# Dilated heads two tokens per transpose, XT reordered in its copy out of PSUM, and no filler matmuls, in a fused attention and soft-MoE kernel

## The chip, the cores and the metric

The kernel runs on one core of one Trainium2 chip. The metric is device time in microseconds (us) for one execution. The engines are TensorE (PE in the profile, with PEld for its weight loads), VectorE (DVE), ScalarE (ACT), GpSimd (POOL) and SyncE (SP). They run side by side and wait for one another by semaphores. POOL issues all input loads here, SP the stores.

## What is computed

Attention with a sliding window, and then a soft mixture of experts on its result. There are 8 batches, 8 heads, 576 tokens and 64 values per head.

```python
scores = scale * np.matmul(q, k.transpose(0, 1, 3, 2))
rel = pos[:, None] - pos[None, :]
mask_plain = (rel >= 0) & (rel < 32)                            # heads 0 to 3
mask_dil = (rel >= 0) & (rel < 128) & (rel % 4 == 0)            # heads 4 to 7
attn_out = softmax(where(mask, scores, -1e9)) @ v
x = attn_out.transpose(0, 2, 1, 3).reshape(4608, 512)           # tokens x (heads, values)

logits = x @ phi                                                # 4608 x 32 slots
d = softmax of logits over tokens;  slot_input = d.T @ x        # 8 experts x 4 slots
h = np.maximum(slot_input[e] @ w1[e], 0.0)                      # 512 -> 1024
slot_out[e] = h @ w2[e]                                         # 1024 -> 512
c = softmax of logits over slots;   out = c @ slot_out          # 4608 x 512
```

A dilated head's query sees only keys whose distance is a multiple of four. If its tokens are regrouped by their index modulo four, it becomes a plain window of 32 within each group of 144 tokens.

## The kernel before

**Units.** The attention is done in eight units u. A unit is one pair of batches and one type of head: even units hold the four plain heads, odd units the four dilated ones (`ty = u % 2`). Its q, k and v are loaded by POOL into one of three staging slots `stg`, 96 rows (q, k, v times batch times a run of 72 tokens) on 96 partitions for each of two halves of the heads.

**Stages of a unit.** Each stage is a call of a function `st_...`, which adds operations to a list.

- `st_T` (four calls per unit): PE transposes `stg` into PSUM against an identity (L515), and ACT copies two banks to `TT` (L532), which holds values on partitions and tokens along the free dimension. For dilated heads the copy puts the tokens in groups modulo four. Two 64-column transposes, one for each half of the heads, fill the two halves of PSUM's partitions. POOL's next load into this staging slot waits for these transposes.
- `st_S` (six calls): scores (L550), ACT's exponential (L557) and DVE's mask (L565) for four blocks of 96 queries against 128 keys, of two heads that lie on the two halves of the partitions. `win` gives the window of `TT` for a block.
- `st_V` (four calls): PE transposes v back (L575), DVE copies it (L580).
- `st_P` (four calls): probabilities times v, with a column of ones for the sum (L603); DVE takes the reciprocal (L612) and scales into `XB` (L614), tokens on partitions.
- `st_X` (four calls): PE transposes `XB` (L631), and DVE or ACT copies it to `XT` (L640, L641), values on partitions. For dilated heads `XT` is in the grouped order of tokens.
- `st_L` (odd units only, once per batch): logits from the `XT` of both types (L660), eight matmuls of 192 and 384 columns. For the dilated half the output goes to PSUM with a step of four, so that its tokens come out in natural order. ACT takes the exponential (L665), DVE copies parts of it (`expX`, L672), PE transposes it per block (L692), DVE copies (`ET`, L696), and PE adds the slot inputs into one PSUM bank (L705).

**Tail.** The slot inputs are copied (L747), folded (L752), copied again (`siT`, L757). Then come the first expert layer (L772), the token sums (L809), a transpose of h (L790) with copies (L799), the second expert layer (L830, in three parts by when weights land), its scaling (L844, L848), and 18 output blocks (L869, copies L872 and L875, stores L880). Expert weights are loaded by POOL into `WD`, and the last nine into `stg` and `TT` as those come free.

**Order.** `Prog.schedule` is a planner. It takes each operation's cost in microseconds, its key (a due time from `due`, units 13.1 us apart) and its dependences, and lays every engine's order down at build time. Calls of neighbouring units interleave. An operation with two engines named (`("dve", "act")`) goes to the one that can start it first. A change of PE's weight shape has a cost of its own in the planner (`mode`). PSUM has seven banks in the planner's pool, of which pairs are taken by most stages. Where PE would stand still for over 0.4 us by the plan and the plan's time is past `FILL[0]`, the planner puts in matmuls whose result nobody reads (`filler`, L889).

## Time and profile before

| | |
|---|---|
| median of 3 runs | 189.43 us |
| lowest of them | 189.08 us |
| the profiled execution | 190.36 us, of which the span from first to last instruction is 188.6 us |
| PE busy | 142.1 us (75%), 2872 matmuls |
| DVE, ACT, POOL busy | 110.1 us, 94.2 us, 35.8 us |
| read from HBM, written | 61.93 MB, 9.44 MB |
| PE's granted clock, mean | 0.926 of full |
| matmuls whose result is unused (L889) | 32, 8.9 us busy |

A row of a group of instructions gives line, engine, operation, output and input with partitions and elements, the count, then busy time and the mean duration of one in ns, and the idle time of the engine before them with its releaser. Rows in order of time give start, length, engine and line. Rows of windows give a stretch, the busy time of the engines in it with counts, the clock granted to PE, the share of the DMA engines' time, and GB/s. The chain is followed back from the last instruction; "issue" in it is time in which an engine waited for nothing that the profile shows.

### The profile page before, as it was taken

The page shows a single profiled execution, that of the slowest core. Times are in us where ns is not written, and L with a number is a line of the kernel's source. Part 1 is how long each engine was busy: PE and PEld are TensorE (multiplying, and loading weights), DVE is VectorE, ACT ScalarE, POOL GpSimd, SP SyncE. Part 2 cuts the span into 40 slices and gives each one's busy share as a digit, 9 for nine tenths or more (in the row PEclk, how much of TensorE's full clock was granted, in tenths as well). Part 3 has the DMA queues.
Part 4 walks back from the last instruction along what each step waited for, and adds up shares of the span by engine and source line. Part 5 has one row for each costly group of instructions (what it writes and reads, how often), then busy time and mean ns, then how long its engine had stood idle before and what let it go on. Part 6 is the DMA issues. An engine that isn't in the chain of part 4 may idle for free.

```text
span 188.6 us, 6342 instructions
## 1 busy us (share of the span) xinstructions
PE 142.1 (75%) x2872; PEld 104.4 (55%) x2872; DVE 110.1 (58%) x256; ACT 94.2 (50%) x136; POOL 35.8 (19%) x72
## 2 busy tenths in 40 slices
PE   0028879599987878998949799887899999996000
PEld 0028668487766757776837677675664658311000
DVE  6820794496687359569528966948943130699000
ACT  2006857456675655675649476478321020699000
POOL 7980603301500420440020020010400000000000
PEclk9999999669999978999996999999699999999855
DMA  5999999999999999999999999949999950199998
GB/s 76 211 215 211 213 212 218 213 216 215 212 210 220 216 208 221 213 212 215 216 216 208 219 219 217 208 99 151 219 215 214 215 109 3 60 405 405 407 403 322
DMA packets 7898, 40.83 MB, mean 216 GB/s; under 512 B 1856, under 2 KB 1856, under 8 KB 4416
## 3 DMA queue, kind: packets, MB, share of 16 engines
q0 software_dynamic: 4752, 30.94, 79.9%
q1 hardware_dynamic: 3120, 9.50, 12.8%
q8 instruction: 22, 0.36, 0.7%
q14 instruction: 4, 0.03, 0.0%
HBM read 61.93 MB, written 9.44 MB: 378 GB/s over the span
## 4 chain that ended last, share of the span: by engine, by line
PE 50%; DVE 26%; issue 5%; DMA 5%; ACT 4%; POOL 1%; DVEq 0%; POOLq 0%
PE ps L515 13%; DVE PT L565 8%; PE ps L660 6%; DVE XB L614 6%; PE ps L631 6%; DVE WD L875 5%; DVE VN L580 5%; DMA stg<-in_v_dram 5%; PE ps L889 4%; PE ps L575 4%; PE ps L603 3%; PE ps L550 3%; PE ps L830 3%; ACT PT L557 2%; PE ps L772 2%
## 5 line engine op out<-in xcount | busy, mean ns | idle before, releaser
L532 ACT ACTIVATE TT<-ps 128x864 f32<-128x864 f32 x32 | 28.3, 894 | 30.0 <-PE ps L515 30.0
L515 PE MATMUL ps<-ident,stg 96*64 96x96 bf16 x1152 | 32.4, 215 | 14.4 <-DMA stg<-in_v_dram 12.9
L557 ACT ACTIVATE PT<-ps 128x768 bf16<-128x768 f32 x48 | 37.4, 810 | 10.0 <-PE ps L550 10.0
L515 PEld LDWEIGHTS ps<-ident,stg 96*64 96x64 bf16 x1152 | 28.3, 116 | 16.6 <-DMA stg<-in_v_dram 12.9
L614 DVE TENSOR_TENSOR XB<-ps,RV 96x768 bf16<-96x768 f32 x32 | 30.2, 945 | 0.5
L580 DVE COPY VN<-ps 128x768 bf16<-128x768 bf16 x32 | 17.6, 549 | 19.2 <-PE ps L575 19.1
L550 PE MATMUL ps<-TT 64*128 64x96 bf16 x384 | 17.9, 221 | 4.5 <-issue 2.5
L603 PE MATMUL ps<-VN,PT 128*128 128x65 bf16 x384 | 19.0, 203 | 2.8 <-DVE VN L580 1.1
L575 PE MATMUL ps<-ident,TT 128*128 128x128 bf16 x192 | 18.4, 238 | 2.3 <-issue 2.3
L603 PEld LDWEIGHTS ps<-VN,PT 128*128 128x128 bf16 x384 | 15.7, 104 | 5.3 <-DVE VN L580 1.5
L396 POOL DMA_DIRECT2D stg<-in_q_dram x16 | 8.4, 526 | 51.3 <-PE ps L515 50.5
L631 PE MATMUL ps<-ident,XB 96*128 96x96 bf16 x192 | 13.6, 214 | 5.1 <-DVE XB L614 3.0
L575 PEld LDWEIGHTS ps<-ident,TT 128*128 128x128 bf16 x192 | 12.5, 107 | 7.9 <-issue 5.3
L631 PEld LDWEIGHTS ps<-ident,XB 96*128 96x128 bf16 x192 | 10.4, 103 | 8.1 <-issue 3.7
L550 PEld LDWEIGHTS ps<-TT 64*128 64x128 bf16 x384 | 10.8, 102 | 7.2 <-ACT PT L557 1.6
L641 ACT ACTIVATE XT<-ps 128x576 bf16<-128x576 bf16 x16 | 10.4, 648 | 8.2 <-PE ps L631 8.2
L640 DVE COPY XT<-ps 128x576 bf16<-128x576 bf16 x16 | 7.3, 455 | 11.4 <-PE ps L631 11.4
L565 DVE TENSOR_TENSOR PT<-PT,mask_d 128x768 bf16<-128x768 bf16 x24 | 12.8, 535 | 0.9 <-ACT PT L557 0.5
L660 PE MATMUL ps<-XT,phi_pad 128*128 128x192 bf16 (+1 forms) x64 | 13.0, 362 | 0.0
L565 DVE TENSOR_TENSOR PT<-PT,mask_p 128x768 bf16<-128x768 bf16 x24 | 12.7, 541 | 0.0
L612 DVE RECIPROCAL RV<-ps 96x12 f32<-96x12 f32 x32 | 7.1, 223 | 7.9 <-PE ps L603 7.8
L425 POOL DMA_DIRECT2D stg<-in_moe_w_dram x6 | 3.2, 534 | 42.1 <-PE ps L515 42.1
(75 smaller groups left out, 161.5 us busy)
## 6 DMA issues: line engine op xcount, KB each, us to landing
WD<-in_moe_w_dram POOLq DMA_DIRECT2D x7, 1024.0 KB, 25.4
out_dram<-WD SPq DMA_DIRECT2D x14, 512.0 KB, 5.0
stg<-in_moe_w_dram POOLq DMA_DIRECT2D x6, 1024.0 KB, 15.2
stg<-in_q_dram POOLq DMA_DIRECT2D x16, 288.0 KB, 13.2
stg<-in_k_dram POOLq DMA_DIRECT2D x16, 288.0 KB, 14.9
stg<-in_v_dram POOLq DMA_DIRECT2D x16, 288.0 KB, 17.5
TT<-in_moe_w_dram POOLq DMA_DIRECT2D x2, 1024.0 KB, 14.5
out_dram<-stg SPq DMA_DIRECT2D x4, 512.0 KB, 5.1
```

The source lines that it names most:

```text
L515: i_ = t.transpose(bankb2(pt, a)[64 * hx:64 * hx + 64, 96 * kk:96 * kk + 96], src[:, hx, c, :], ident[0:96, 0:96])
L532: return ac.activation(d, sv, ACTF.Copy)
L550: i_ = t.matmul(pair(sc)[:, hx, QB * x:QB * x + QB], win(u, 1, h01, blk_, bpar)[64 * hx:64 * hx + 64], win(u, 0, h01, blk_, bpar)[64 * hx: ...
L557: op("act", lambda ac: ac.activation(sbt(pt)[:, 0:768].rearrange("p (x n) -> p x n", x=2), pair(sc)[:, :, 0:384], ACTF.Exp, scale=SCALE), ...
L565: return dv.tensor_tensor(p_, p_, m.unsqueeze(1).to_broadcast([128, 2, 384]), AluOp.mult)
L575: i_ = t.transpose(bankb(pv)[:, 128 * m:128 * m + 128], win(u, 2, h01, m, bpar), ident[:, :])
L580: op("dve", lambda dv: dv.tensor_copy(sbt(vn)[:, :, :, 0:64], bankb(pv)[:, 0:768].rearrange("p (m x d) -> p m x d", m=6, x=2)), r=[pv], w= ...
L603: i_ = t.matmul(pair(po)[:, hx, 65 * m:65 * m + 65], sbt(pts[i])[:, o_:o_ + 128], sbt(vn)[:, m, hx, 0:65], start=True, stop=True)
L614: op("dve", lambda dv: dv.tensor_tensor(sbt(xb)[:].rearrange("p m (x h d) -> p h x m d", x=2, h=2)[:, h01], pv()[:, :, :, 0:64], sbt(rv)[: ...
L631: i_ = t.transpose(bankb(px)[:, QB * m:QB * m + QB], sbt(xb)[:, m, 128 * x:128 * x + 128], ident[0:QB, 0:QB])
L641: return en.activation(d, s_, ACTF.Copy)
L660: i_ = t.matmul(o_, phi_pad[:, c].rearrange("p j i -> p (j i)"), rhs, start=c == 0, stop=c == 3)
```

## The change

It has three parts, and new costs for the planner.

1. In odd units `st_T` transposes 96 x 128 at a time: two tokens next to each other in one head, 18 transposes per call instead of 36. The halves of the partitions then hold even and odd tokens instead of two heads. `win` finds its windows accordingly, ACT's copy goes to one half of `TT`, and `st_P` puts its results at the places in PSUM from which `XB` gets the same layout of values.
2. The copy of a dilated `XT` out of PSUM reads with a step and writes in a row, so that `XT` is in natural order. The logits' matmuls then read and write in a row for both types. The steps in `expX` and in the transposes of the exponential (L692) follow the new order of blocks.
3. `FILL[1]` is zero, so the planner puts in no filler.

```diff
-FILL = (125.0, 1e9)
+FILL = (125.0, 0)
...
     def win(u, t, h01, i, bpar):
-        base = (2 * t + h01) * S + QB * i - (HALO if t else 0)
+        if u % 2 == 0:
+            base = (2 * t + h01) * S + QB * i
+        else:
+            base = (6 * (i // 3) + 2 * t + h01) * 288 + QB * (i % 3)
+        base -= HALO if t else 0
...
     def st_T(u, j):
+        two = stg[0:96, s, :].rearrange("r (x c d) -> r x c d", x=2, d=128)
...
                 for kk in range(9):
-                    c = 18 * j + 9 * a + kk if ty == 0 else 4 * (9 * a + kk) + j
+                    if ty:
+                        c = 2 * (9 * a + kk) + j % 2
+                        i_ = t.transpose(bankb2(pt, a)[:, 96 * kk:96 * kk + 96],
+                                         two[:, j // 2, c, :], ident[0:96, 0:96])
+                        continue
+                    c = 18 * j + 9 * a + kk
...
-        op("pe", pe, r=[b_id, b_stg[s]], w=[pt], alloc=[pt], cost=0.86, mode="h",
+        op("pe", pe, r=[b_id, b_stg[s]], w=[pt], alloc=[pt], cost=0.86 if ty == 0 else 0.75,
+           mode="h" if ty == 0 else "f",
...
-                d = t32.rearrange("p (s n) -> p s n", s=6)[:, :, 144 * j:144 * j + 144]
+                d = t32[:, 1728 * (j // 2):1728 * (j // 2) + 1728].rearrange(
+                    "p (s n) -> p s n", s=6)[:, :, 144 * (j % 2):144 * (j % 2) + 144]
...
     def st_P(u, g):
-                for hx in range(2):
-                    o_ = 384 * hx + QB * x
-                    i_ = t.matmul(pair(po)[:, hx, 65 * m:65 * m + 65],
+                for half in range(2):
+                    o_ = 384 * half + QB * x
+                    bk, po_ = (half, m) if ty == 0 else (m // 3, 3 * half + m % 3)
+                    i_ = t.matmul(pair(po)[:, bk, 65 * po_:65 * po_ + 65],
...
     def st_X(u, bpar, x):
             d, s_ = sbt(xt)[:, x, :], bankb(px)[:, 0:S]
+            if ty:
+                s_ = s_.rearrange("p (y x s) -> p s x y", y=2, x=2)
+                d = d.rearrange("p (s x y) -> p s x y", y=2, x=2)
...
-           cost={"dve": 0.38, "act": 0.55}, key=k0 + 0.6)
+           cost={"dve": 0.38 if ty == 0 else 0.8, "act": 0.57}, key=k0 + 0.6)
...
     def st_L(b, u):
-                    if c < 2:
-                        rhs = sbt(x0)[:, c, lo:hi]
-                    else:
-                        o_ = o_.rearrange("p (i r) -> p r i", r=4)
-                        rhs = sbt(x1)[:, c - 2, :].rearrange("p (r i) -> p r i", r=4)[
-                            :, :, lo // 4:hi // 4]
+                    rhs = sbt((x0, x1)[c // 2])[:, c % 2, lo:hi]
...
-                n = expT[:, S * b:S * b + S].rearrange("p (i x y) -> p x y i", x=2, y=2)
+                n = expT[:, S * b:S * b + S].rearrange("p (i y x) -> p x y i", x=2, y=2)
...
-                    f_ = QB * m
-                    o_ = 4 * (f_ % 144) + f_ // 144
+                    o_ = m // 3 + (4 * 48 + 2 if m % 3 else 0)
```

The planner's costs also change for the scores (0.2 to 0.22), L603 (0.41 to 0.46), L631 (0.28 to 0.31), L692 (0.5 to 0.56) and L752 (1.4 to 1.9). These numbers alter no instruction, only the order that the planner lays down.

## Prediction

> **What bounds the kernel now.** I read the page first: the slices, then the chain that ended last.

> ```profile
> span 188.6 us, 6342 instructions
> ...
> DMA  5999999999999999999999999949999950199998
> ...
> PE 50%; DVE 26%; issue 5%; DMA 5%; ACT 4%; POOL 1%; DVEq 0%; POOLq 0%
> ```

> The DMA engines are full almost throughout, yet half of the chain is PE. Two holes in the DMA line (slice 27, and 33 to 35) reconcile this. I asked for the first by a window and by order of time.

> ```profile
> 122.00:127.00 5.00, 4.38 (x140) 3.78 (x139) 2.67 (x5) 3.75 (x5) 0.38 (x1) 1.00 0.57 118
> ...
> 126.62 1.06 POOL L425 DMA_DIRECT2D stg<-in_moe_w_dram  x2 [15.65 <-PE ps L515]
> ...
> 163.54 15.62 SPq L880 DMA_DIRECT2D out_dram<-WD  x14
> ```

> The first row gives the stretch, the five engines' busy time, PE's clock, the DMA share and GB/s: over those five microseconds DMA moves at 0.57. The queue runs dry because the weights that go into unit 7's staging slot cannot be issued before unit 7's transposes (L515) are done, at 126.6. The second hole lies ahead of the first store at 163.54, where PE finishes the expert layers with every weight on the chip. After it comes only output, 188.6 - 163.5 = 25 us of DMA that the change leaves alone. So the end is set by when PE gets through eight units of attention and the tail behind them; loading fits around it. A microsecond less on PE is a microsecond less at the end, as long as DVE and ACT keep up.

> **The change part by part.** *Logits (L660).* Half of a batch's eight matmuls write PSUM with a step of four today; afterwards all write in a row.

> ```profile
> 45.99 1.64 PE L660 MATMUL ps<-XT,phi_pad 128*128 128x192 bf16 x8
> ...
> 47.41 0.46 PE L631 MATMUL ps<-ident,XB 96*128 96x96 bf16 x6
> ...
> 145.50 1.04 PE L889 MATMUL ps<-mask_p,ident 128*128 128x512 bf16 x4
> ...
> L889 PE MATMUL ps<-mask_p,ident x32: 376/379/634, 136.0 to 161.8; 128*128 128x512 bf16 x32
> ```

> From the first logits matmul to the next group's start is 47.41 - 45.99 = 1.42 us for 4 x 192 + 4 x 384 = 2304 columns, 0.62 ns each. The unused matmuls, which write in a row, give the other price: four span 1.04, less the last one's own 0.379, over three steps: 0.22 us per 512 columns, 0.43 ns each, or 0.99 us for 2304. That is 0.43 us a batch and 3.4 us for eight. Bounds: nothing (if the step in PSUM isn't the reason) and 3.4.

> *Transposes of the dilated heads (L515).* A call of 36 transposes from 64-column weights becomes 18 from 128-column weights, a shape that XB's transposes (L631) have already.

> ```profile
> 121.06 0.96 PE L515 MATMUL ps<-ident,stg 96*64 96x96 bf16 x36
> ...
> 121.99 0.43 PE L631 MATMUL ps<-ident,XB 96*128 96x96 bf16 x6
> ...
> 122.35 0.96 PE L515 MATMUL ps<-ident,stg 96*64 96x96 bf16 x36
> ...
> 123.24 0.43 PE L631 MATMUL ps<-ident,XB 96*128 96x96 bf16 x6
> ...
> L515 PE MATMUL ps<-ident,stg 96*64 96x96 bf16 x1152 | 32.4, 215 | 14.4 <-DMA stg<-in_v_dram 12.9
> ...
> L631 PE MATMUL ps<-ident,XB 96*128 96x96 bf16 x192 | 13.6, 214 | 5.1 <-DVE XB L614 3.0
> ```

> Steps within a group: (0.96 - 0.215)/35 = 21.3 ns now, so 36 take 0.77 us; (0.43 - 0.214)/5 = 43 ns in the new shape, so 18 take 0.78. The transposes themselves gain nothing. But each change of weight shape costs: L515 to L631 takes 123.24 - 122.35 = 0.89 where 0.77 is work, L631 to L515 0.36 where 0.26 is work, so about 0.11 per switch. A dilated unit's four calls lie between calls with full weights (unit 7 here), except where the next unit's call follows: six switches vanish per unit, 24 in all, 24 x 0.11 = 2.6 us, less 16 x 0.01: I take 2.4, bounds 0 and 2.6.

> *XT in natural order from the copy.* The copies of the dilated half (16 of 32) now read PSUM with a step.

> ```profile
> L640 DVE COPY XT<-ps 128x576 bf16<-128x576 bf16 x16 | 7.3, 455 | 11.4 <-PE ps L631 11.4
> ...
> L532 ACT ACTIVATE TT<-ps 128x864 f32<-128x864 f32 x32 | 28.3, 894 | 30.0 <-PE ps L515 30.0
> ...
> L875 DVE TENSOR_SCALAR stg<-ps,rtok 128x512 f32<-128x512 f32 x4 | 2.7, 740 | 0.0
> ```

> [...] In the middle of the run ACT, whose waits on L515 alone are 30 us, takes most of them: cost 0 there, up to 16 x 0.35 = 5.6 if no cover held. In the tail, the copy at 136.26 (below) holds the logits: +0.35. No DMA, queue or semaphore is moved by the change.

> *No unused matmuls (L889).* These rows are the chain near the tail; the last three are DVE by time.

> ```profile
> 136.22 1.31 PE ps L889 x4
> ...
> 142.42 0.44 PE ps L705 x12
> 142.86 0.97 PE ps L889 x4
> 143.83 0.58 PE ps L692 x12
> 144.41 0.66 PE ps L889 x3
> 145.07 0.50 PE ps L705 x12
> 145.57 0.97 PE ps L889 x4
> ...
> 154.40 1.08 PE ps L889 x5
> ...
> 159.09 0.54 PE ps L889 x2
> ...
> 136.26 0.46 DVE L640 COPY XT<-ps 128x576 bf16<-128x576 bf16 x1
> ...
> 154.44 0.42 DVE L799 COPY hT<-ps 128x64 bf16<-128x64 bf16 x2 [0.18 <-PE ps L790]
> ```

> What would be late instead? At 136.22 the XT copy, until 136.72, so of 1.31 some 0.7 is freed. At 154.40 the copy of hT until 154.86: 0.55 freed. At 159.09 nothing: 0.54 freed. In the three pieces between 142.86 and 146.54 PE waits for copies that end as late as the fillers do: nothing, perhaps 0.1. Sum 1.9 us freed, bounds 1.1 and 2.6 (another 0.7 if the remaining pieces hide less than they seem).

> Against it stands PE's clock. Seven windows, cut where the clock changed (stretch, busy time, clock, DMA):

> ```profile
> 17.53:20.94 3.41, 2.42 (x70) 1.00 1.01 210
> ...
> 31.18:34.60 3.42, 1.77 (x53) 1.00 1.02 214
> 34.60:38.01 3.41, 2.92 (x40) 0.50 1.04 216
> 38.01:41.42 3.41, 3.41 (x54) 0.50 1.00 208
> ...
> 130.17:133.58 3.41, 1.77 (x42) 1.00 1.04 219
> 133.58:137.00 3.42, 3.33 (x39) 0.50 1.03 216
> 137.00:140.41 3.41, 3.37 (x33) 1.00 1.04 216
> ```

> After a window with 1.77 of 3.42 busy (52%) the next ran at half clock; after 2.42 (71%) it did not; and a window at half clock with 2.92 (86%) was followed by another at half, one with 3.33 (97%) by full clock. Without fillers the 4.12 us from 142.42 to 146.54 hold 0.44 + 0.58 + 0.50 = 1.52 of work, 37%: I expect half clock there, and it lasts through the fold (L752, 1.88 us) into the first expert layer (L772, 3.57 us) until one window is nearly full. One window at half clock loses up to 3.4/2 = 1.7; the fold, with its gaps, about 0.9 more: +2.6. Bounds: 0, if it stays up, and half of both and the window after, 5.2.

> [...]

> *Order and the other engines.* Fewer microseconds on PE only count where PE is the late one.

> ```profile
> 84.45 0.33 DVE L672 COPY expX<-expT 128x96 bf16<-128x96 bf16 x2 [1.21 <-ACT expT L665]
> ...
> 85.01 0.56 DVE L580 COPY VN<-ps 128x768 bf16<-128x768 bf16 x1 [0.23 <-PE ps L575]
> ```

> DVE's long stretches begin like this: it waits for PE (0.23) and, just before, for the exponential of the logits (1.21), which comes earlier too. So nearly all of the saving gets through; I give back a tenth of 3.4 + 2.4, 0.6. The planner's new costs order the calls anew; I count that as nothing, bounds 1.2 either way.

> **Sum.** -3.4 - 2.4 + 0.35 - 1.9 + 2.6 + 0.6 = -4.15, rounded to -3.9 for switches that the new order brings back. The profiled execution took 190.4 us (span 188.6 and 1.8 around it), so 186.5 in its terms; the median of the runs shown is 189.43, 0.9 lower, so 185.5.

> **The rivals.** *The tail stays at full clock.* Without the 2.6 it ends at 182.9. [...] Against: the 52% rows.

> *The gain is swallowed.* DVE and ACT, with dearer copies, become the late ones in each pair of units; half of 5.8 is lost and the time is about 188.4. For it: 26% of the chain is DVE. Against: DVE loses copies to ACT. The stall below gives nearly the same time if it strikes in the tail:

> ```profile
> 67.43 0.33 PE L575 MATMUL ps<-ident,TT 128*128 128x128 bf16 x3 [2.33 <-issue]
> ```

> PE stands still there in mid-group, for nothing that the profile shows. One more such stall between 142 and 160 costs 2.3: 187.8.

> *Slower.* The half clock lasts through the tail: +5.2 instead of 2.6, and the step in PSUM was not what made the logits slow (+3.4 back), or the copies' 5.6 has no cover. It decides from the point where PE's share in the windows of the tail never reaches some nine tenths before the second expert layer: 185.5 + 2.6 + 3.4 = 191.5, and 193 or more with the copies.

> *Not what it says.* If the copy costs as much more as the matmul saves, the step has only moved: that is the swallowed case.

> **How the numbers follow.** Forecast (184 to 187.2) 0.45; full clock (182 to 184) 0.17; swallowed (187.2 to 190) 0.26; slower (above 190) 0.12. The range 182.0 to 190.0 leaves 0.15 or so out. Two per cent, about what a measurement here can tell from no change, is 185.64 and 193.2: faster takes the full clock and somewhat over half of the forecast, 0.46; slower by over 2% only the worst of the last case, 0.08; the rest, 0.46, is within.

> **What would show it.** L660: eight matmuls in about 1.0 us from first start to the next group. L515 in odd units: 18 per call at 43 ns, and the next group about 0.78 us after the first. L640 for dilated heads near 0.8 us, and few of them. No L889. Unit 7's L515 ends some 4 us earlier (near 122), and the DMA hole of slice 27 is gone. PE's clock at half somewhere between 142 and 150, with L752 and L772 longer. Wrong would be: L660 still 1.4 us, DVE late at every logit, or the first expert layer at full clock.

## The result, and the profile after

The median went from 190.22 us (189.43 without one run of 641 us) to 183.24 us (182.48 to 183.72): a ratio of 0.965, with a 95% interval of 0.957 to 0.973. The profiled execution took 182.93 us, with a span of 181.2 instead of 188.6: 7.4 us less. Some executions are slower as a whole and stay out of the ratios; among them are nearly all runs of two experiments below (unused matmuls out of before, many small pads) and the profiled run of a third (transposes alone), so the first two have no ratio and these three traces are read for single events only.

From the page of the kernel after, the slices and the chain:

```profile
span 181.2 us, 5690 instructions
...
DMA  5999999999999999999999999999999981699995
...
DVE 26%; DMA 25%; PE 23%; ACT 8%; POOL 6%; issue 3%; DVEq 0%; POOLq 0%
```

DMA holds a quarter of the chain, where it held 5%, and PE a quarter instead of half. The hole of slice 27 is gone: the DMA line is full until every weight is there. The chain itself, kernel after, start, length and what:

```profile
71.84 1.09 PE ps L671 x8
...
75.46 0.99 PE ps L671 x8
...
122.21 1.04 POOL TT L425 x2
123.25 27.74 DMA TT<-in_moe_w_dram
```

The last weight is issued at 122.21 and lands at 150.99, and PE's second expert layer waits for it. The rows in order of time, kernel after (line numbers shift: L515 is now L520 for dilated and L525 for plain heads, L631 L644, L640 L656, L660 L671, L752 L762, L772 L782, L809 L819, L830 L840, L880 L890):

```profile
56.66 0.93 PE L520 MATMUL ps<-ident,stg 96*128 96x96 bf16 x18
57.42 0.42 PE L644 MATMUL ps<-ident,XB 96*128 96x96 bf16 x6
57.68 0.93 PE L520 MATMUL ps<-ident,stg 96*128 96x96 bf16 x18
...
115.82 1.06 POOL L425 DMA_DIRECT2D stg<-in_moe_w_dram  x2 [13.73 <-PE ps L520]
...
124.60 0.75 DVE L656 COPY XT<-ps 128x576 bf16<-128x576 bf16 x1
...
137.31 1.04 PE L782 MATMUL ps<-WD,siT 128*32 128x512 bf16 x7 [0.58 <-DVE siT L767]
...
143.47 1.05 PE L819 MATMUL ps<-rowm,expT 128*128 128x1 bf16 x36
...
151.03 1.92 PE L840 MATMUL ps<-TT,hT 128*32 128x256 bf16 x16 [1.76 <-DMA TT<-in_moe_w_dram]
...
155.01 15.62 SPq L890 DMA_DIRECT2D out_dram<-WD  x14
```

Cut at two marks, the last load into unit 7's slot and the first store, the 7.4 us divide so:

| | before | after | |
|---|---|---|---|
| unit 7's transposes done | 126.6 | 115.8 | -10.8 |
| from there to the first store | 36.9 | 39.2 | +2.3 |
| first store to the end | 25.1 | 26.2 | +1.1 |

So three things are to be explained: why PE gained 10.8 us by unit 7 where about 4 were forecast, why 2.3 came back in the tail, and why output that the change leaves alone takes a microsecond longer.

**A theory for the first.** The stalls put down to "issue" have a rhythm. Kernel before, rows in order of time, and then the windows from the end of one stall to the start of the next (the 67.43 row of the prediction belongs to them):

```profile
35.09 0.56 PE L631 MATMUL ps<-ident,XB 96*128 96x96 bf16 x5 [2.14 <-issue]
...
61.30 0.74 PE L515 MATMUL ps<-ident,stg 96*64 96x96 bf16 x26 [0.90 <-issue]
...
98.48 0.20 PE L550 MATMUL ps<-TT 64*128 64x96 bf16 x1 [2.52 <-issue]
```

```profile
29.00:32.78 3.78, 3.75 (x127) 3.42 (x128) 1.64 (x3) 2.63 (x5) 1.42 (x3) 1.00 1.02 213
61.28:64.92 3.64, 3.62 (x127) 3.28 (x128) 1.52 (x3) 2.35 (x3) 1.21 (x3) 1.00 1.00 210
92.34:95.80 3.46, 3.44 (x127) 3.18 (x128) 1.41 (x4) 2.35 (x4) 0.94 (x2) 1.00 1.01 209
```

Each window ahead of a long stall holds 128 weight loads and 127 recorded matmuls (taken here as 128 with one record missing): 256 instructions of PE, used up in 3.5 to 3.8 us. From the start of such a window to the end of the stall behind it are 35.09 - 29.00 = 6.09 us, 67.43 - 61.28 = 6.15, and 98.48 - 92.34 = 6.14. A transfer of another kind falls into each; queues of the DMA engines, kernel before, 28 to 36 us:

```profile
q8 instruction: 1, 0.02, 0.7%
```

```profile
62.33:68.70 6.37, 5.23 (x128) 3.98 (x128) 6.01 (x13) 5.01 (x7) 1.26 (x3) 1.00 0.99 206
```

lasts 6.37 us, and no stall follows. PE's waits put down to issue, before and then after, line, total, times, longest:

```profile
PE ps L550 <- issue: 2.5, 1, 2.5
PE ps L575 <- issue: 2.3, 1, 2.3
PE ps L631 <- issue: 2.1, 1, 2.1
PE ps L515 <- issue: 1.1, 2, 0.9
```

```profile
PE ps L525 <- issue: 2.3, 3, 1.0
```

8.0 us became 2.3. Around the end of each of the three long stalls, from 0.5 us ahead of it to 1.3 us behind, a stretch at half clock begins (34.60 to 41.42, 68.73 to 72.14, 99.45 to 102.86: 13.6 us); up to unit 7 the kernel after has 3.4 us of that (43.62 to 47.03). So a stall can cost more than its own length; how much was not measured. **The rival** was that transposes with full weights are cheaper in PE's own time by more than was reckoned.

### The profile page after: what moved, and what is told of

The parts are those of the page before. It is cut to its first block, busy times and chain, and to the rows that moved or that the text cites. A ratio compares the mean times of both kernels' runs of the same rounds, so it can differ in the third digit from the quotient of the medians.

```text
span 181.2 us, 5690 instructions
## 1 busy us (share of the span) xinstructions
PE 128.8 (71%) x2551; PEld 96.6 (53%) x2552; DVE 112.9 (62%) x257; ACT 93.1 (51%) x135; POOL 35.8 (20%) x72
## 3 DMA queue, kind: packets, MB, share of 16 engines
q0 software_dynamic: 4752, 30.94, 82.6%
HBM read 61.93 MB, written 9.44 MB: 394 GB/s over the span
## 4 chain that ended last, share of the span: by engine, by line
DVE 26%; DMA 25%; PE 23%; ACT 8%; POOL 6%; issue 3%; DVEq 0%; POOLq 0%
DMA TT<-in_moe_w_dram 15%; DMA stg<-in_v_dram 10%; DVE XB L627 8%; DVE PT L577 6%; DVE WD L885 5%; ACT PT L569 5%; POOL stg L396 4%; PE ps L671 4%; PE ps L520 3%; DVE VN L592 3%; PE ps L587 3%; PE ps L525 3%; PE ps L562 2%; PE ps L644 2%; ACT TT L544 2%
## 5 line engine op out<-in xcount | busy, mean ns | idle before, releaser
L525 PE MATMUL ps<-ident,stg 96*64 96x96 bf16 x576 | 17.0, 219 | 17.5 <-DMA stg<-in_v_dram 13.2
L525 PEld LDWEIGHTS ps<-ident,stg 96*64 96x64 bf16 x576 | 14.9, 119 | 19.1 <-DMA stg<-in_v_dram 13.4
L616 PE MATMUL ps<-VN,PT 128*128 128x65 bf16 x384 | 17.6, 194 | 2.9 <-DVE PT L577 1.4
L656 DVE COPY XT<-ps 128x576 bf16<-128x576 bf16 x17 | 10.1, 596 | 12.2 <-PE ps L644 12.1
L587 PE MATMUL ps<-ident,TT 128*128 128x128 bf16 x192 | 16.5, 224 | 0.7 <-DVE VN L592 0.5
L562 PE MATMUL ps<-TT 64*128 64x96 bf16 x384 | 15.4, 205 | 2.1 <-ACT TT L544 1.0
L644 PE MATMUL ps<-ident,XB 96*128 96x96 bf16 x192 | 13.6, 215 | 3.6 <-DVE XB L627 3.6
L520 PE MATMUL ps<-ident,stg 96*128 96x96 bf16 x288 | 14.9, 206 | 0.1
L644 PEld LDWEIGHTS ps<-ident,XB 96*128 96x128 bf16 x192 | 10.5, 103 | 5.9 <-DVE XB L627 4.9
L587 PEld LDWEIGHTS ps<-ident,TT 128*128 128x128 bf16 x192 | 11.1, 99 | 4.5 <-DVE VN L592 1.4
L520 PEld LDWEIGHTS ps<-ident,stg 96*128 96x128 bf16 x288 | 13.0, 98 | 0.3 <-ACT PT L569 0.3
L879 PE MATMUL ps<-so_sb,expT 128*128 128x512 bf16 x35 | 10.3, 384 | 1.5 <-ACT so_sb L858 0.8
```

Of the source, the lines that this page charges most:

```text
L520: i_ = t.transpose(bankb2(pt, a)[:, 96 * kk:96 * kk + 96], two[:, j // 2, c, :], ident[0:96, 0:96])
L525: i_ = t.transpose(bankb2(pt, a)[64 * hx:64 * hx + 64, 96 * kk:96 * kk + 96], src[:, hx, c, :], ident[0:96, 0:96])
L562: i_ = t.matmul(pair(sc)[:, hx, QB * x:QB * x + QB], win(u, 1, h01, blk_, bpar)[64 * hx:64 * hx + 64], win(u, 0, h01, blk_, bpar)[64 * hx: ...
L587: i_ = t.transpose(bankb(pv)[:, 128 * m:128 * m + 128], win(u, 2, h01, m, bpar), ident[:, :])
L616: i_ = t.matmul(pair(po)[:, bk, 65 * po_:65 * po_ + 65], sbt(pts[i])[:, o_:o_ + 128], sbt(vn)[:, m, half, 0:65], start=True, stop=True)
L644: i_ = t.transpose(bankb(px)[:, QB * m:QB * m + QB], sbt(xb)[:, m, 128 * x:128 * x + 128], ident[0:QB, 0:QB])
```

## The experiments

**Transposes alone.** The kernel before with two tokens per transpose; logits, copy of XT, unused matmuls and the planner's other costs stay as they were (against the kernel after, the main lines):

```diff
-FILL = (125.0, 0)
+FILL = (125.0, 1e9)
...
-            if ty:
-                s_ = s_.rearrange("p (y x s) -> p s x y", y=2, x=2)
-                d = d.rearrange("p (s x y) -> p s x y", y=2, x=2)
...
+                    if c < 2:
+                        rhs = sbt(x0)[:, c, lo:hi]
+                    else:
+                        o_ = o_.rearrange("p (i x y) -> p y x i", x=2, y=2)
+                        rhs = sbt(x1)[:, c - 2, :].rearrange("p (y x i) -> p y x i", x=2, y=2)[
+                            :, :, :, lo // 4:hi // 4]
```

> Before, with the two-token transposes of the dilated heads alone (logits still written with a step, copies of XT in a row, fillers kept). Two theories. Pages: PE gets its instructions in pages of 256 and needs about 6 us for the next page while loads run; a transpose call of 72 instructions in 0.8 us empties a page in 3.5 us, and PE then stands still for 2.1 to 2.5 us, three times in the kernel before, each time followed by half clock. With half the instructions these three stalls go: unit 7's transposes end 6 to 8 us earlier (near 119 instead of 126.6), the time falls by 5 to 6 us to a ratio of 0.97. Switches alone, as the prediction had it: 24 switches of 0.1 us, 2.4 us less, ratio 0.987, and the three stalls stay.

Median 187.17 us (184.5 to 189.31), ratio 0.971 (0.962 to 0.980). Rows in order of time:

```profile
43.53 0.87 PE L525 MATMUL ps<-ident,stg 96*64 96x96 bf16 x32 [0.75 <-issue]
...
98.22 0.78 PE L616 MATMUL ps<-VN,PT 128*128 128x65 bf16 x19 [0.48 <-issue]
...
104.50 0.70 PE L525 MATMUL ps<-ident,stg 96*64 96x96 bf16 x24 [1.26 <-issue]
121.25 1.07 POOL L425 DMA_DIRECT2D stg<-in_moe_w_dram  x2 [14.68 <-PE ps L520]
```

These are the three stalls that its rows put down to issue up to unit 7; the long ones are gone. Unit 7's transposes end at 121.25, 5.4 us earlier than before, where the switches alone would give 2.4. Near 119 was expected, so the pages' share is smaller here than thought. Up to unit 7 the waits put down to issue fell from 8.0 to 2.5 us. PE still ran at about half its pace for a while: 36 transposes of plain heads (L525) took 1.65 us at 70.29 and at 72.64, where they took 0.96 at 59.81.

**XT in natural order alone.** The kernel before with the reordering copy and logits that write in a row:

```diff
+            if ty:
+                s_ = s_.rearrange("p (r i) -> p i r", r=4)
+                d = d.rearrange("p (i r) -> p i r", r=4)
...
+                    rhs = sbt((x0, x1)[c // 2])[:, c % 2, lo:hi]
```

> Before, with the natural order of XT from its copy alone (64-column transposes, fillers kept). PE issues as many instructions as before. Pages: eight logits matmuls take 1.0 us instead of 1.4, unit 7's transposes end some 2.5 us earlier, the three stalls of over 2 us stay, and the time falls by about 3 us, ratio 0.983. Rival, that a shorter PE order alone makes the stalls go: 7 us or more less, ratio under 0.965. Rival, that the dearer copies on DVE take it back: ratio 0.995 or above, with logits waiting for the copies.

Median 187.45 us, ratio 0.983 (0.977 to 0.988).

```profile
66.44 0.23 PE L575 MATMUL ps<-ident,TT 128*128 128x128 bf16 x1 [2.53 <-issue]
...
97.39 0.38 PE L575 MATMUL ps<-ident,TT 128*128 128x128 bf16 x4 [2.30 <-issue]
...
123.61 1.05 POOL L425 DMA_DIRECT2D stg<-in_moe_w_dram  x2 [14.31 <-PE ps L515]
```

The long stalls stay where the dense transposes stay (a third, of 2.13 us, ends at 35.06). Unit 7 is done 3.0 us earlier, near the 2.6 of six batches' logits at 0.43. With the 5.4 above that makes 8.4 of the 10.8, and no run places the other 2.4. The waits put down to issue grew here, from 8.0 to 10.7 us in all: the stalls took back part of what the logits gave, which can be why the two parts together gain more than their sum. The planner's new costs, which no run has by themselves, are another candidate. And single traces differ: a second one of the kernel after ends unit 7 at 114.65 where the first has 115.82.

**Pads: many small instructions, or few long ones.** The kernel after, with work on PE that nobody reads in each of the sixteen dilated calls: first 18 matmuls of one column (36 instructions), then one fp32 matmul of 32 columns (4 instructions: 2 matmuls in its rows and a weight load to each, as the fp32 fold L752 shows 8 and 8), which took 0.21 us a call, too little to compare, then two of them (8 instructions):

```diff
+                        i_ = t.matmul(pair(pt)[:, a, 440:441], ident[:, :], ident[:, 0:1],
+                                      start=True, stop=True)          # many, each transpose
...
+                        if (a, kk) == (1, 8):                         # few, once or twice a call
+                            i_ = t.matmul(pair(pt)[:, a, 440:472],
+                                          phi_st[:].rearrange("p c s -> p (c s)"), fold[:],
+                                          start=True, stop=True)
```

> After, with 18 one-column matmuls more in every transpose call of the dilated heads (their results are read by nobody): 36 instructions of PE more per call, as many as before had, for some 18 x 25 ns = 0.45 us of PE's time. To be read against pad_few, which adds about the same time with 4 instructions. Pages: the pages that these calls use up last under 6 us again, the stalls at page ends in the first 120 us come to 3 us or more beyond those of pad_few, and unit 7's transposes end 3 us or more later than there. Rival, that only PE's time counts: both alike within 0.7 us.

> After, with one float32 matmul of 32 columns more in every transpose call of the dilated heads (its result is read by nobody): 4 instructions of PE more per call, 2 x 0.233 = 0.47 us of PE's time by the fold's row. Both theories: 16 x 0.47 = 7.4 us more on PE, unit 7's transposes near 122 instead of 115.8; the time 4 to 6 us above after, since the last expert's weight comes 2 us before PE would be ready for it. The stalls at page ends stay near those of after.

> As pad_few, with two float32 matmuls per call instead of one. In pad_few one cost 0.21 us per call and not 0.47, while the 18 one-column matmuls of pad_many cost 0.49, so the two were unlike in PE's time. Two should cost about 0.68 us per call, more than pad_many's, with 8 instructions instead of 36. Pages: unit 7's transposes still end 4 us or more ahead of those of pad_many (128.3), at 118 to 123, and the time stays under 186. Rival, that PE's time alone made pad_many slow: they end later than pad_many's, and the time is as long as there or longer, 189 to 193.

Many: median 193.16 us (188.55 to 196.94). One: 181.40 us, ratio 0.948 (0.939 to 0.957); its forecast, 4 to 6 us above the kernel after, was wrong. Its 16 x 0.21 = 3.4 us on PE delayed nothing: unit 7 is done at 115.20. Two: 181.68 us (181.31 to 182.04), ratio 0.953 (0.947 to 0.960). Rows in order of time, the kernel with many pads and then that with two long ones:

```profile
35.23 0.37 PE L646 MATMUL ps<-ident,XB 96*128 96x96 bf16 x5 [1.02 <-issue]
...
42.02 0.39 PE L618 MATMUL ps<-VN,PT 128*128 128x65 bf16 x7 [0.72 <-issue]
...
48.42 0.38 PE L589 MATMUL ps<-ident,TT 128*128 128x128 bf16 x4 [1.26 <-issue]
...
128.34 1.07 POOL L425 DMA_DIRECT2D stg<-in_moe_w_dram  x2 [15.19 <-PE ps L522]
```

```profile
57.08 0.93 PE L520 MATMUL ps<-ident,stg 96*128 96x96 bf16 x18
57.84 0.60 PE L524 MATMUL ps<-fold,phi_st 128*128 128x32 f32 x4
58.27 0.54 PE L621 MATMUL ps<-VN,PT 128*128 128x65 bf16 x12
...
118.79 1.07 POOL L425 DMA_DIRECT2D stg<-in_moe_w_dram  x2 [15.30 <-PE ps L524]
```

Two long pads take 58.27 - 57.84 = 0.43 us in a call (0.68 was expected), 16 x 0.43 = 6.9 us in all. The many small ones take a step of 70 ns where a transpose alone takes 43, so 18 x 0.027 = 0.49 us a call and 7.8 in all. Nearly the same PE time, and unit 7 is done 118.79 - 115.82 = 3.0 us later with 8 more instructions a call and 12.5 us later with 36. In the latter the stalls come back, one page apart (42.02 - 35.23 = 6.8, 48.42 - 42.02 = 6.4): its waits put down to issue come to 5.5 us, against 2.3 in the kernel after, 2.2 with one long pad and 1.9 with two. And its fastest run, 188.55, is 6.5 us above the slowest with two long pads, 182.04. That speaks for the pages and against the rival. By the theory a page that lasts 6 us costs nothing, and one of 3.5 us costs the rest; PE's own time is partly covered by other engines anyway, since 6.9 us of it moved unit 7 by 3.0. The size of the 12.5 is not to be taken as that of the stalls: PE's mean granted clock is 0.899 in that trace and 0.939 in the one with two long pads.

**Unused matmuls out of before, and back into after.** `FILL[1]` alone, each way; the second was run twice, the other time beside a second run of the kernel after:

```diff
-FILL = (125.0, 1e9)
+FILL = (125.0, 0)         # in before; the reverse in after
```

> Before, without the fillers and nothing else. By the prediction's step: 1.9 us freed where no wait hides the fillers, 2.6 us lost because PE runs at half clock through the first expert layer; +0.7, ratio 1.004, with that layer at about 6 us instead of 3.6. Rival, that the clock stays up: ratio 0.99. Unit 7's transposes end where they did, near 126.

> After, with the fillers back. If loading sets the end now (the last weight lands at 151.0 and the last expert waits for it): the same time as after, within 0.5 us, the first expert layer at 3.6 us and the last expert's wait for its weight longer by 1 us or more than the 2.0 us of after. If PE's tail still set the end: 0.7 us or more less than after, with no longer wait for the weight.

Out of before: median 194.06 us (190.63 to 195.76) beside 191.43 (189.94 to 194.72). Whether it is slower stays open, since its fastest run, 190.63, lies among those of before. Windows of its tail, and one piece of its chain:

```profile
146.30:149.70 3.40, 1.87 (x27) 1.49 (x27) 1.51 (x5) 0.00 (x0) 0.00 (x0) 0.99 1.03 217
...
153.10:156.50 3.40, 3.40 (x40) 1.25 (x36) 0.00 (x0) 0.60 (x1) 0.00 (x0) 0.50 0.65 126
```

```profile
151.75 5.95 PE ps L772 x54
```

Without them a window with 1.87 of 3.40 busy is followed by two at half clock, of which the second is shown, and the first expert layer takes 5.95 us instead of the 3.57 before. There it is on the chain of this trace.

Back into after: 181.98 us, ratio 0.954 (0.949 to 0.960): 1.3 us faster than the kernel after as first timed. The pair on one chip:

> The changed kernel unaltered, as the measure for fill_again on the same chip: a ratio of 0.955 to 0.973 to before.

> After with the fillers back, a second time, beside after itself. If loading alone sets the end: equal within 0.5 us. If PE's tail at half clock still comes in now and then, since it ended only 2.0 us ahead of the last weight: 0.5 to 1.5 us less than after, and never more.

183.12 us (182.46 to 184.28) without, 181.91 (181.42 to 182.91) with; ratios 0.961 (0.955 to 0.968) and 0.956 (0.950 to 0.961). 1.2 us less by the medians, though the intervals of the ratios touch. The two traces differ by 1.8: the first stores lie at 155.95 and 155.12, and output takes 26.05 and 25.08.

**One weight load less.** Expert 3's first layer uses expert 2's weight, so 2.1 MB less is read (59.83 instead of 61.93), and part of the result differs; once without the unused matmuls and once with them:

```diff
-    W_AFTER = {2: ["w10"], 3: ["w11"], 4: ["w12"], 5: ["w13"], 6: ["w14"],
+    W_AFTER = {2: ["w10"], 3: ["w11"], 4: ["w12"], 6: ["w14"],
...
+    w1v[3] = w1v[2]
```

> After, without loading expert 3's first weight (its first layer uses expert 2's weight, so part of the result differs): 2.1 MB or 4.9 us less to load, PE's work the same. If loading sets the end: PE no longer waits for the last weight, and the time falls by those 2.0 us and no further, since PE's tail (half clock in the first expert layer) ends at 149.0 and sets it then. If PE set the end already: no change, within 0.5 us.

> As no_w13, with the fillers back. Now that loading is out of the way, the fillers have their price: by the prediction's step -2.6 for half clock in the first expert layer and +1.9 for the fillers' own time, so some 0.7 us less than no_w13. If the clock were worth nothing: 1.9 us more.

180.92 us (178.61 to 182.03), ratio 0.937 (0.925 to 0.950), and 179.98 (179.76 to 180.46), ratio 0.940 (0.933 to 0.948). The chain of the first:

```profile
136.55 5.14 PE ps L783 x36
...
143.75 5.01 PE ps L841 x128
```

No wait for a weight is left: PE runs the second expert layer through in 5.01 us, and the first store is at 150.80 instead of 155.01. Unit 7 is done at 115.75, as in the kernel after (115.82). Of the 4.2 us, 2.4 are this layer without its wait (it took 152.97 - 145.60 = 7.37 us with it), and 1.8 its earlier start, behind a first layer of 5.14 us instead of 6.16 and less half clock (a mean granted clock of 0.943 against 0.922). The second part isn't what was left out, so only the 2.4 speak for the load stream. Which of the two versions is faster isn't settled: medians and ratios point opposite ways. In the traces the first store comes at 150.80 without the unused matmuls and at 153.07 with them (1.0 of this lies ahead of unit 7's end), though DVE's wait for the first expert layer (L783) is 4.0 us with them, the same as in before, where that layer takes 3.57, and 5.3 without. So their forecast gain of 0.7 is not seen.

**The last page early.** Output takes 25.06 to 25.15 us from the first store in the kernel before and in ten of the twelve experiments, and 26.2, 26.1 and 26.1 in the kernel after, its second trace, and the version without expert 3's load and without unused matmuls. Only in these three does the fetch of an instruction page fall into the output. DMA queues and issues from 155 to 181 us, kernel after (KB each, median us to landing):

```profile
q8 instruction: 1, 0.02, 0.2%
...
out_dram<-WD SPq DMA_DIRECT2D x14, 512.0 KB, 6.4
```

This fetch starts at 161.0, 6.0 us behind the first store. By the theory its place goes by the number of instructions that PE has used up, and the unused matmuls shift it by theirs. If that is their worth, anything that shifts it does as well; 64 matmuls of one column at the start, where PE waits for the first load:

```diff
+    def pe_lead(t):
+        for _ in range(64):
+            i_ = t.matmul(bank(lead)[:, 0:1], ident[:, :], ident[:, 0:1], start=True, stop=True)
+        return i_
+    op("pe", pe_lead, r=[b_id], w=[lead], alloc=[lead], cost=2.0, key=-1)
```

> After, with 64 one-column matmuls (128 instructions, read by nobody) at the very start, where PE waits for the first load anyway. They move the ends of PE's instruction pages by half a page. In after and after_again the last page was fetched during the output (at 161.0 and 156.8), and from the first store to the end took 26.2 and 26.0 us; wherever that fetch came ahead of the first store it took 25.1. If the fetch costs the output that microsecond: the last page is fetched before the first store, the output takes 25.1 us, and the time is 1 us below after, 181.9 to 182.4. If it is the missing fillers or the clock that cost it: 26 us again, and the time of after, 183.1.

181.78 us (181.58 to 182.55), ratio 0.956 (0.951 to 0.960). The same view, 155 to 181 us, has no row of that kind:

```profile
out_dram<-WD SPq DMA_DIRECT2D x14, 512.0 KB, 5.0
```

A store lands after 5.0 us instead of 6.4, and from the first store (154.69) to the end (179.8) are 25.1 us. It is faster than the kernel before, and its median is 1.3 to 1.5 us below the kernel after's (183.24 and 183.12), though their ratio intervals touch. The versions with long pads (181.4, 181.68) or the unused matmuls (181.91, 181.98) lie within 0.4 us of it, with output of 25.1 as well; no run tells which of these five versions is the fastest. How a fetch of 16 KB goes with a whole microsecond more of output was not tried.

## Why the prediction was right or wrong

It forecast 185.5 us in a range of 182.0 to 190.0; 183.24 lies in the range, 2.3 below the forecast. That is outside the likeliest case's own 184 to 187.2, in the interval of the rival "the tail stays at full clock", which did not come true. So the sum was off, by errors that partly cancel: unit 7 was done 10.8 us earlier where some 4 were forecast, and 3.4 of that were lost again, 2.3 up to the first store and 1.1 in the output. That the time fell into the range is partly luck.

- **The bound, right for before, wrong for after.** "A microsecond less on PE is a microsecond less at the end" and "loading fits around it" held for the first microseconds only. The last weight lands at 150.99, PE waits 1.76 us for it, and of 10.8 us gained by unit 7 some 8.5 arrive at the first store. The step that failed is that no floor was worked out for the load stream. An estimate from the page and the windows of before: its queue carries 30.94 MB, at 208 to 219 GB/s that takes 141 to 149 us, whatever PE does.
- **Logits: right.** Batches of 1.09 and 0.99 us on the chain, where 1.42 was measured from start to next group before; 0.99 and 0.43 saved were the terms.
- **Weight shapes: right in themselves.** From one call's first transpose to the next group are 57.42 - 56.66 = 0.76 us (0.78 expected; 0.89 before), and back 0.26 instead of 0.36. But the step counted the change in PE's time and not in its **instructions**, and this is the term that was mis-sized: the transposes alone moved unit 7 by 5.4 us, not 2.4.
- **The rival with the 2.33 us stall.** It said that PE stands still "for nothing that the profile shows", and feared one more. The profile did show it: the same 6.1 us from the start of a dense stretch to the end of its stall, 256 instructions, and a transfer of its own kind. Read so, fewer instructions should have been expected to lessen it.
- **XT's copy.** 0.75 us on DVE, 0.3 more than the 0.455 of a copy in a row. The summand of +0.35 is 0.8, the planner's cost for it in the diff, less that 0.455. No run shows the 0.8: it was the author's estimate, between two rows of before, the 0.455 of L640 and 740 x 576/512 = 0.83 at the pace of the float32 copy L875. "Few of them" was wrong. The groups of the kernel after, count, busy time, mean ns, idle time before them:

```profile
L656 DVE COPY XT<-ps 128x576 bf16<-128x576 bf16 x17 | 10.1, 596 | 12.2 <-PE ps L644 12.1
L657 ACT ACTIVATE XT<-ps 128x576 bf16<-128x576 bf16 x15 | 9.8, 650 | 3.6 <-PE ps L644 3.3
```

  The copies stay shared, and idle time ahead of both groups shows that PE is the late one there, as the step assumed.
- **Half clock in the tail: right in size, wrong in worth.** Windows of the kernel after:

```profile
132.30:135.80 3.50, 2.06 (x23) 1.67 (x21) 1.24 (x2) 0.00 (x0) 0.00 (x0) 1.00 1.01 211
135.80:139.20 3.40, 2.82 (x24) 1.57 (x28) 0.45 (x2) 0.00 (x0) 0.00 (x0) 0.50 1.08 226
139.20:142.60 3.40, 3.40 (x40) 1.27 (x32) 0.00 (x0) 0.60 (x1) 0.00 (x0) 0.50 0.99 207
```

  59% busy, then two windows at half clock, the first 83% busy and the second full, and then full clock again, as in the prediction's seven windows. As a rule it has exceptions: the kernel after's window from 149.43 to 152.84 is 53% busy (1.81 of 3.41), and full clock follows. The first expert layer takes 143.47 - 137.31 = 6.16 us, 2.6 more than 3.57, which was the price, though the prediction put 0.9 of it into the fold, which took 2.08 us instead of 1.88. But behind it PE still waits 1.76 us for a weight that lands when it lands, so the last wait covered it here. With one long pad that layer's matmuls take 539 to 548 ns each (379 to 380 in before), and the first store comes at 154.54 all the same.
- **No unused matmuls: the loss of 0.7 is not shown.** That was 1.9 freed against 2.6 lost. Taken out of before, the loss stays open. In the kernel after they are worth 1.2 us by the medians, but 1.0 us between the two traces (26.05 against 25.08) goes with the page in the output, which no step had; and with that page moved the kernel without them takes 181.78 us, against 181.91 and 181.98 with them.
- **Unit 7 near 122, and slice 27.** The hole went, as said; the time was 115.8.

## What to carry to other kernels

Where a bound is one engine's and a stream stands close behind it, work out the stream's own floor before counting a gain in full. Count instructions as well as microseconds: where a wait put down to nothing comes back after the same number of instructions, look for a fetch, since halving the instructions was worth more here than the busy time told. Where an edit leaves a phase alone and that phase still changes, look for a transfer that has moved into it.

## What the runs showed of the hardware that was not expected

- In three places of before, 256 instructions of PE took about 6.1 us with the stall behind them (6.09, 6.15 and 6.14), beside a load stream of 209 to 213 GB/s. Each time a dense stretch of 3.5 to 3.8 us was followed by a stall of 2.1 to 2.5 us, in which one 16 KB instruction transfer lay.
- One 16 KB instruction fetch during 25.1 us of stores goes with about 1 us more (26.05 to 26.2 in three traces with one, 25.06 to 25.15 in eleven without), and with stores that land after 5.9 to 6.4 us instead of 5.0.
- PE's clock halved behind windows of which little more than half was busy: 1.87 us of 3.40 (before without the unused matmuls) and 2.06 of 3.50 (the kernel after) were followed by half clock, though 1.81 of 3.41 (the kernel after) once was not. The longest single wait in the first two windows is 0.80 us.
